# Filters of a Fourier mixer loaded over 128 partitions instead of 64

## The chip, the cores and the metric

The kernel runs on one core of a Trainium2 chip. The metric is the device time of one launch in microseconds (us). A core has five instruction queues that run side by side: TensorE (PE in the profile; PEld is its weight load), VectorE (DVE), ScalarE (ACT), GpSimd (POOL) and SyncE (SP). SP does no arithmetic; in this kernel it issues the plain DMA transfers, which 16 DMA engines carry out. Data lies in SBUF, which has 128 partitions; matmul results arrive in PSUM banks and are moved to SBUF ("evacuated") by DVE or ACT.

## The reference, cut to what matters

```python
# x: 8 batches x 2496 positions x 256 channels; filt_r, filt_i: 1249 frequencies x 256
X = np.fft.rfft(x, axis=1)
Y = X * (filt_r + 1j * filt_i)          # a complex filter for each frequency and channel
y = np.fft.irfft(Y, n=2496, axis=1)     # 19968 rows of 256
# then a mixture of 8 experts: each row goes to the expert with the largest gate logit
h = np.maximum(rows_of_e @ w1[e], 0.0)  # 256 -> 1024
out = gate * (h @ w2[e])                # 1024 -> 256
```

All of it is float32. The change concerns only how the filter gets into SBUF, which happens once, in the first 50 us.

## The kernel before, in words

The length 2496 is split as 39 x 64, so that a transform is a matmul with a 39-point table, a matmul with a 64-point table, the product with the filter, and the two inverse tables. A batch passes four stages: A (table `tas`, from x), B (table `tbs`, then the filter), C (table `tcs`) and D (table `tds`). Batch 0 keeps its intermediate results in SBUF and turns them with TensorE transposes; batches 1 to 7 go through DRAM between the stages (`zd` after A, `ud` after C). x is laid out in 22 columns of 128 partitions a batch and read in six chunks (`load_x`, L506): five of 512 KB and one of 256 KB. The expert products begin later, between the stages of the following batches, and fill most of the span.

After stage B's matmul a PSUM bank holds, for two of the `NF` = 20 frequency slots f, the real part on partitions 0 to 63 and the imaginary part on partitions 64 to 127. `stage_b` (L542) multiplies it on DVE and adds:

```python
nc.vector.tensor_mul(ys, z2, ht[:, f:f + 2, :])             # both halves times filt_r
... yw[:HP] = -z2[HP:] * fi ; yw[HP:] = z2[:HP] * fi        # crosswise times filt_i
nc.gpsimd.tensor_tensor(ys, ys, yw, op=ALU.add)             # batch 0, at times up to batch 2; else on DVE
```

So `filt_r` is needed alike on both halves, and `filt_i` on one half only, whose index is `f // 10`: `fi` for slots 0 to 9 lies on partitions 0 to 63, and for slots 10 to 19 on partitions 64 to 127. The tile `ht` (L366) holds both: columns 0 to 19 are `filt_r`, columns 20 to 29 are `filt_i` folded in this way. The filter in DRAM has the same shape (128 x 30 x 256), with `filt_r` present twice. For part of the frequencies `filt_i` must change its sign; the signs are in `sgs`, and GpSimd multiplies them in.

`load_filters(c)` (L419) is called five times, for chunks of four slots, each time between two chunks of `first_a` (L612, stage A of batch 0). It issues DMAs on SP and puts the sign products on a list. `turn_z(f)` (L628, the transposes between stage A and B of batch 0) starts, at every fourth f, with the copy of `filt_r` from the lower half to the upper on ACT, and with the sign products of the chunks up to one ahead.

What sets the order of the work: a planner written into the kernel (class `Order`) keeps an estimated clock for each engine, and picks the next step by when its inputs and banks are expected; all instructions are recorded through one helper, which is why nearly every row of the profile has the line L246. `Order.parts` (L152) splits `ht` into pieces for this estimate. `either` (L401) gives an evacuation to DVE or ACT, whichever is expected to end first. `more_loads` (L1288) issues the loads of x, `zd` and `ud`, at most seven tiles at a time (tile name `fin`). SP issues its DMAs strictly in order, and each waits for the landing of the eighth before it, besides what it needs itself.

Of the kernel before, what the change touches and what calls it, by code (L numbers as in the profile page):

```python
# [19 lines left out]
P = 128  # L20
S = 2496
D = 256
# [6 lines left out]
NF = (N1 + 1) // 2  # L29
# [95 lines left out]
class Order:  # L125
# [25 lines left out]
    @staticmethod  # L151
    def parts(a):  # L152

        if a.name[:3] != "ht_":
            return [a.name]
        row, at = divmod(a.offset, a.ap[0][0])
        return [f"{a.name}/{h}/{k}" for h in ((0, 1) if a.ap[0][1] == P else (row // (P // 2),))
                for k in range(at // (2 * D), at // (2 * D) + (a.ap[1][1] + 1) // 2)]

    @staticmethod  # L160
    def run(ap):
# [132 lines left out]
def kernel(  # L294
# [16 lines left out]
    nc = Order(tc.nc)  # L311
# [13 lines left out]
    for b in range(B):  # L325
        GROUPS.append([])
        for rows, most in WANT[b]:
            n = min(most, max(0, ((b + 1) * S - (N - left) - E * (rows - 1)) // rows))
# [35 lines left out]
    sgs = cst.tile([P, NF // 2], F32, name="sgs")  # L364

    ht = cst.tile([P, NF + NF // 2, D], F32, name="ht")  # L366
# [28 lines left out]
    def bank():  # L395
        return ps.tile([P, 512], F32, tag="bank", name="bank")
# [12 lines left out]
    def evac(o, i, n):  # L409
        either(i, n, lambda: nc.vector.tensor_copy(o, i), lambda: nc.scalar.copy(out=o, in_=i))  # L410

    HP = P // 2
# [4 lines left out]
    signs = []  # L417

    def load_filters(c):  # L419
        f0, n = FH[c]  # L420
        if c == 0:
            nc.sync.dma_start(out=tbs, in_=tb)
            nc.sync.dma_start(out=sgs, in_=sg)
        nc.sync.dma_start(out=ht[:HP, f0:f0 + n], in_=filt[:HP, f0:f0 + n, :])
        half, f1 = divmod(f0, NF // 2)
        rows = slice(half * HP, (half + 1) * HP)
        nh = min(n, NF // 2 - f1)
        parts = [(rows, slice(f1, f1 + nh), slice(NF + f1, NF + f1 + nh))]
        if nh < n:
            parts.append((slice(HP, P), slice(0, n - nh), slice(NF, NF + n - nh)))  # L430
        for r, fs, at in parts:
            nc.sync.dma_start(out=ht[r, at], in_=filt[r, at, :])
            signs.append((c, ht[r, at], sgs[r, fs, None].to_broadcast((HP, fs.stop - fs.start, D))))
        if c == 0:
            nc.sync.dma_start(out=tcs, in_=tcm)

# [190 lines left out]

    def turn_z(f):  # L628
        if f % 4 == 0:
            nc.scalar.copy(out=ht[HP:, f:f + 4], in_=ht[:HP, f:f + 4])  # L630
            while signs and signs[0][0] <= f // 4 + 1:
                _, part, sign = signs.pop(0)
                nc.gpsimd.tensor_tensor(part, part, sign, op=ALU.mult)
        zi = outs["zi", f] = pro.tile([P, 2, D], F32, tag="zi", name="zi")
        p = bank().rearrange("p (i h d) -> p i h d", i=2, h=DH)
        for i in range(2):
            for h in range(DH):
                nc.tensor.transpose(p[:, i, h, :], zu["z"][:, h, f + i].rearrange("p t c -> p (t c)"), ident)
        evac(zi, p.rearrange("p i h d -> p i (h d)"), 2 * D)
# [576 lines left out]
    def slot(k):  # L1216

        steps, nch = [], len(CH)
        if k == 0:
            steps.append((0.8, load_rest, None, 0.0, None))  # L1220
            for f in range(-2, NF + 2, 2):
                at = (f + 2) / (NF + 4)
                if 0 <= f < NF:
                    steps.append((at, lambda f=f: stage_b(k, f), None, 0.85, "b", lambda f=f: count("y") < 4 and [outs["zi", f]]))
                if f + 2 < NF:
                    steps.append((at + 0.01, lambda f=f: turn_z(f + 2), None, 0.44, "z", lambda: count("zi") < 2 and [zu["z"]]))
                if f >= 2:
                    steps.append((at + 0.02, lambda f=f: first_c(f - 2), None, 0.85, "c", lambda f=f: [outs["y", 0, f - 2]]))
        elif k < B:
            for f in range(0, NF + 4, 2):  # L1230
                at = f / (NF + 4)
                if f < NF:
                    steps.append((at, lambda f=f: stage_b(k, f), ("z", k, f // 4) if f % 4 == 0 else None, 0.85, "b", lambda f=f: count("y") < 4 and [ins["z", k, f // 4]]))
                if f >= 4:
                    steps.append((at + 0.01, lambda f=f: stage_c(k, f - 4), None, 0.85, "c", lambda f=f: [outs["y", k, f - 4], 0.0 if f % 4 else sb.free("st") - 0.9]))
# [31 lines left out]
        return sorted(steps, key=lambda step: step[0])  # L1267

    STEPS = [(0.0, lambda: load_filters(0), None, 0.0, None)]
    for c in range(len(CH)):  # L1270
        STEPS.append((0.0, lambda c=c: first_a(c), ("x", 0, c), 0.43 * CH[c][1], None))
        if c + 1 < len(FH):
            STEPS.append((0.0, lambda c=c: load_filters(c + 1), None, 0.0, None))
# [191 lines left out]
    with tc.manual_schedule(engines=None):  # L1465
# [4 lines left out]
        fs = list(STEPS)  # L1470
# [103 lines left out]
```

## Time and profile before

| what | value |
|---|---|
| three runs | 1468.29, 1470.89, 1471.23 us; median 1470.89 us |
| the profiled execution's own time | 1474.5 us |
| its span, first to last instruction | 1472.8 us |
| mean granted TensorE clock | 0.992 |
| HBM read / written | 196.45 MB / 80.64 MB |
| busy: DVE, ACT, POOL | 835.8, 480.5, 818.9 us |
| filter loads (`ht<-in_filt_dram`) | 11 DMAs from 8.5 to 28.0 us: nine of 256 KB, two of 128 KB |

How to read the profile: times are us from the first instruction; a row `out<-in` names the tile written and the tiles read; "idle before" is how long the engine had nothing to run, with the one that released it. The chain of waits follows the last instruction back to what let it start, again and again, so its pieces are the stretches that set the end. PEclk in a table of windows is the share of full clock that TensorE was granted. GB/s is what the 16 DMA engines moved together.

### The profile page before, as it was taken

How to read it: one execution, taken by the hardware profiler on the slowest of the kernel's cores; microseconds unless marked ns; L12 is line 12 of the kernel's file. 1: busy time of each engine (PE TensorE's matmuls, PEld its weight loads, DVE VectorE, ACT ScalarE, POOL GpSimd, SP SyncE). 2: the span in 40 equal slices, each digit the busy share in tenths (PEclk: the TensorE clock that was granted, in tenths of full speed). 3: DMA queues.
4: the chain of work that ended last, by engine and by line, in shares of the span. 5: the costliest groups of instructions: out<-in, count | busy, mean ns of one | idle time of the engine just before them, and what ended most of it. 6: DMA issues, size and time to landing. Idle time of an engine off the chain costs nothing.

```text
span 1472.8 us, 25703 instructions
## 1 busy us (share of the span) xinstructions
PE 1438.4 (98%) x7828; PEld 1148.5 (78%) x7828; DVE 835.8 (57%) x1818; ACT 480.5 (33%) x1005; POOL 818.9 (56%) x1214
## 2 busy tenths in 40 slices
PE   8998999999999999999999999999999999999998
PEld 5553555777577777777787778889999999999997
DVE  4666568335766574566757554566878775531110
ACT  3553443233232333222223232222232322223332
POOL 3434355525456654565375567647989878831111
PEclk9999999999999999999999999999999999999999
DMA  9749798887786576557345644548665424456661
GB/s 255 243 156 339 250 323 257 271 260 222 246 246 189 169 253 180 150 167 251 105 126 151 205 117 132 149 128 244 175 186 154 133 77 139 135 191 176 173 192 42
DMA packets 216383, 278.19 MB, mean 189 GB/s; under 512 B 124131, under 2 KB 163708, under 8 KB 216245
## 3 DMA queue, kind: packets, MB, share of 16 engines
q1 hardware_dynamic: 197125, 233.19, 53.7%
q0 software_dynamic: 19120, 43.33, 8.5%
q8 instruction: 66, 1.08, 0.3%
q14 instruction: 72, 0.59, 0.1%
HBM read 196.45 MB, written 80.64 MB: 188 GB/s over the span
## 4 chain that ended last, share of the span: by engine, by line
PE 85%; DMA 6%; DVE 4%; issue 2%; POOL 1%; SPq 1%; ACT 1%; POOLq 0%; DVEq 0%; ACTq 0%
PE bank L246 85%; DMA fin<-in_x_dram 2%; DMA fin<-ud 2%; DVE yw L246 1%; DVE ys L246 1%; DMA ud<-uo 1%; DMA fin<-zd 1%; SPq L246 1%; POOL out_dram L246 0%; DVE hT L246 0%; DMA w1t<-in_moe_w_dram 0%; DMA ng<-rows 0%; ACT hT L246 0%; DMA zd<-zo 0%; DMA xg<-rows 0%
## 5 line engine op out<-in xcount | busy, mean ns | idle before, releaser
L246 DVE TENSOR_TENSOR hT<-bank,hT 128x512 f32<-128x512 f32 (+1 forms) x504 | 300.8, 626 | 165.4 <-PE bank L246 77.7
L246 PE MATMUL bank<-w2t,hT 128*128 128x256 f32 (+1 forms) x1984 | 387.5, 350 | 2.4 <-DVE hT L246 1.4
L246 PEld LDWEIGHTS bank<-w2t,hT 128*128 128x128 f32 x1984 | 335.1, 190 | 53.0 <-issue 11.7
L246 PE MATMUL bank<-xT,w1t 128*128 128x256 f32 (+1 forms) x1728 | 316.3, 329 | 0.2 <-DVE hT L246 0.2
L246 POOL DMA_INDIRECT out_dram<-ys,ng x161 | 161.5, 1003 | 271.6 <-ACT ys L246 136.7
L246 PEld LDWEIGHTS bank<-xT,w1t 128*128 128x128 f32 x1728 | 265.4, 192 | 32.4 <-issue 8.3
L246 ACT ACTIVATE hT<-hT 128x1024 f32<-128x1024 f32 (+1 forms) x144 | 135.0, 959 | 390.5 <-DVE hT L246 387.5
L246 POOL DMA_INDIRECT rows<-yo,row x176 | 181.9, 1034 | 74.8 <-POOL yo L246 38.5
L246 ACT ACTIVATE ys<-bank,ng 128x256 f32<-128x256 f32 x104 | 49.3, 474 | 303.9 <-PE bank L246 235.2
L246 PE MATMUL bank<-sums,wsum 128*128 128x256 f32 (+1 forms) x576 | 135.6, 358 | 0.0
L246 PE MATMUL bank<-w2s,hT 128*128 x592 | 132.6, 379 | 0.0
L246 PEld LDWEIGHTS bank<-w2s,hT 128*128 128x128 f32 x592 | 110.3, 190 | 13.8
L246 PEld LDWEIGHTS bank<-sums,wsum 128*128 128x128 f32 x576 | 100.5, 190 | 17.7 <-issue 6.8
L246 POOL TENSOR_TENSOR wsum<-w1t 128x256 f32<-128x256 f32 x72 | 56.5, 785 | 82.2 <-PE bank L246 57.7
L246 DVE STREAM_TRANSPOSE xT<-xg 128x512 f32<-128x512 f32 (+2 forms) x126 | 57.4, 493 | 54.6 <-PE bank L246 51.4
L246 DVE TENSOR_TENSOR ys<-bank,ht 128x512 f32<-128x512 f32 x80 | 54.8, 685 | 52.2 <-PE bank L246 42.9
L246 PE MATMUL bank<-fin,tas 117*120 117x512 f32 x154 | 77.3, 622 | 6.9 <-DMA fin<-in_x_dram 6.7
L246 PE MATMUL bank<-fin,tds 120*128 120x512 f32 (+1 forms) x168 | 76.1, 573 | 3.9 <-DMA fin<-ud 3.3
L246 PE MATMUL bank<-fin,tbs 128*128 128x512 f32 x140 | 72.6, 605 | 5.4 <-DMA fin<-zd 5.4
L246 PE MATMUL bank<-ys,tcs 128*128 128x512 f32 x140 | 73.3, 611 | 4.2 <-DVE yw L246 3.4
L246 ACT ACTIVATE hT<-bank 128x128 f32<-128x128 f32 (+1 forms) x191 | 57.6, 303 | 52.5 <-PE bank L246 42.9
L246 PE MATMUL bank<-xT,wsum 128*128 128x256 f32 (+1 forms) x288 | 67.8, 358 | 0.2 <-ACT yo L246 0.2
(171 smaller groups left out, 1766.6 us busy)
## 6 DMA issues: line engine op xcount, KB each, us to landing
w1t<-in_moe_w_dram SPq DMA_DIRECT2D x126, 512.0 KB
w2t<-in_moe_w_dram SPq DMA_DIRECT2D x68, 512.0 KB
fin<-in_x_dram SPq DMA_DIRECT2D x39, 512.0 KB
fin<-zd SPq DMA_DIRECT2D x35, 512.0 KB
ud<-uo SPq DMA_DIRECT2D x35, 512.0 KB
fin<-ud SPq DMA_DIRECT2D x35, 512.0 KB
zd<-zo SPq DMA_DIRECT2D x35, 480.0 KB
xg<-rows SPq DMA_DIRECT2D x112, 128.0 KB
```

The lines of the kernel that those rows point to most:

```text
L246: return real(*args, **named)
```

## The change

`filt_r` is loaded onto all 128 partitions by DMA (512 KB a chunk instead of 256 KB), and ACT no longer copies it from the lower half. `filt_i` is loaded on all 128 partitions too, so a load of slots f brings the slots f + 10 with it: the three first chunks load it (512, 512 and 256 KB) and the last two load none. The signs are multiplied on 128 partitions, in three instructions instead of six. `Order.parts` no longer tells the halves of `ht` apart. `filt`, `ht` and `stage_b` stay as they are.

```diff
@@ class Order: parts
-        row, at = divmod(a.offset, a.ap[0][0])
-        return [f"{a.name}/{h}/{k}" for h in ((0, 1) if a.ap[0][1] == P else (row // (P // 2),))
-                for k in range(at // (2 * D), at // (2 * D) + (a.ap[1][1] + 1) // 2)]
+        at = a.offset % a.ap[0][0]
+        return [f"{a.name}/{k}" for k in range(at // (2 * D), at // (2 * D) + (a.ap[1][1] + 1) // 2)]
@@ load_filters
-        nc.sync.dma_start(out=ht[:HP, f0:f0 + n], in_=filt[:HP, f0:f0 + n, :])
-        half, f1 = divmod(f0, NF // 2)
-        rows = slice(half * HP, (half + 1) * HP)
-        nh = min(n, NF // 2 - f1)
-        parts = [(rows, slice(f1, f1 + nh), slice(NF + f1, NF + f1 + nh))]
-        if nh < n:
-            parts.append((slice(HP, P), slice(0, n - nh), slice(NF, NF + n - nh)))
-        for r, fs, at in parts:
-            nc.sync.dma_start(out=ht[r, at], in_=filt[r, at, :])
-            signs.append((c, ht[r, at], sgs[r, fs, None].to_broadcast((HP, fs.stop - fs.start, D))))
+        nc.sync.dma_start(out=ht[:, f0:f0 + n], in_=filt[:, f0:f0 + n, :])
+        nh = max(0, min(n, NF // 2 - f0))
+        if nh:
+            fs, at = slice(f0, f0 + nh), slice(NF + f0, NF + f0 + nh)
+            nc.sync.dma_start(out=ht[:, at], in_=filt[:, at, :])
+            signs.append((c, ht[:, at], sgs[:, fs, None].to_broadcast((P, nh, D))))
@@ turn_z
-            nc.scalar.copy(out=ht[HP:, f:f + 4], in_=ht[:HP, f:f + 4])
```

How the two built kernels compare, instruction by instruction: TensorE's list is the same. SP issues 8 filter loads instead of 11, in the same places between the other loads, which keep their order. ACT loses its five copies of `ht`. The planner's estimates shift a little with that, and `either` gives three evacuations of batches 0 and 1 to ACT that DVE had before. GpSimd has three sign products instead of six. In the kernel before the first two of them stand ahead of the sums `ys` of slots 0 and 2, two more ahead of those of slots 4 and 6, one ahead of slot 8 and one ahead of slot 12; in the changed kernel the first two stand at the same place and the third ahead of slot 4. Everything else on the five lists is the same and in the same order.

## Prediction

> **What bounds the kernel now.** I read the page first: section 1 (busy time) and section 4 (the chain that ended last). TensorE is busy 98% of the span and makes up 85% of the chain; no other engine makes up more than 4%.
>
> ```profile
> PE 1438.4 (98%) x7828; PEld 1148.5 (78%) x7828; DVE 835.8 (57%) x1818; ACT 480.5 (33%) x1005; POOL 818.9 (56%) x1214
> ...
> PE 85%; DMA 6%; DVE 4%; issue 2%; POOL 1%; SPq 1%; ACT 1%; POOLq 0%; DVEq 0%; ACTq 0%
> ```
>
> So taking work off ACT or GpSimd is worth nothing by itself. It counts only where it shortens a wait of TensorE. The filter is used from 19 us on and is complete by about 48 us; so I asked for the chain in order of time, up to 60 us.
>
> ```profile
> 8.48 3.76 PE bank L246 x32
> 12.24 10.14 DMA fin<-in_x_dram
> 22.38 0.14 issue
> 22.52 28.65 PE bank L246 x124
> ...
> 52.26 3.57 DMA zd<-zo
> ...
> 55.98 3.94 DMA fin<-zd
> ```
>
> The columns are start, length, what. One load stands out: `fin<-in_x_dram`, the second x chunk of batch 1. SP issues it at 12.24, and it lands at 22.38, 10.14 us later. TensorE stood idle for 2.92 us before it ("22.52 ... [2.92 <-DMA fin<-in_x_dram]" in the timeline). From 22.52 to 51.17 the chain is TensorE alone. The waits for `zd` at 52 to 60 are behind an ACT evacuation and SP, and begin from TensorE's results.
>
> Why 10 us for 512 KB? The busy times by window tell (columns: busy PE, PEld, DVE, ACT, POOL with counts, then PEclk, DMA share, GB/s):
>
> ```profile
> 8.00:12.00 4.00, 3.52 (x31) 3.52 (x32) 0.95 (x3) 1.13 (x3) 0.00 (x0) 1.00 1.01 398
> 12.00:16.00 4.00, 4.00 (x38) 4.00 (x38) 1.91 (x5) 1.59 (x5) 0.00 (x0) 1.00 1.08 234
> 16.00:20.00 4.00, 3.60 (x20) 2.19 (x18) 1.54 (x4) 2.41 (x5) 0.38 (x1) 1.00 1.03 226
> 20.00:24.00 4.00, 1.48 (x2) 0.80 (x3) 0.48 (x1) 0.41 (x1) 1.51 (x1) 0.73 1.03 224
> ...
> 60.00:64.00 4.00, 3.94 (x15) 2.26 (x16) 2.75 (x4) 1.07 (x2) 0.54 (x1) 1.00 1.03 409
> ```
>
> The DMA engines are full in all five rows. But with 128-partition loads alone (8 to 12 us: x; 60 to 64: x and `zd`) they move 398 and 409 GB/s, and once the 64-partition filter loads are among them, 224 to 234. The second thing to see is PEclk, which I asked for around the idle time:
>
> ```profile
> 18.39:21.80 3.41, 1.21 (x9) 0.80 (x7) 1.29 (x2) 1.73 (x3) 1.89 (x1) 1.00 1.03 214
> 21.80:28.63 6.83, 6.11 (x8) 2.48 (x9) 0.56 (x1) 2.21 (x3) 1.89 (x1) 0.50 1.05 245
> 28.63:58.00 29.37, 29.37 (x152) 19.45 (x150) 23.36 (x36) 17.63 (x34) 18.50 (x14) 1.00 0.70 185
> ```
>
> After 18.39 to 21.80, with TensorE busy for only 1.21 of 3.41 us, the clock is halved for 6.83 us. After 28.63 TensorE is busy without a gap to 58. Two later windows, for comparison:
>
> ```profile
> 124.20:127.62 3.42, 1.38 (x3) 0.30 (x2) 3.32 (x6) 1.45 (x3) 1.53 (x3) 1.00 1.03 339
> ...
> 260.74:264.15 3.41, 1.75 (x4) 0.42 (x3) 2.01 (x10) 2.38 (x9) 0.19 (x1) 1.00 1.00 330
> ```
>
> **The change part by part.**
>
> *Bytes.* Before: nine loads of 256 KB and two of 128 KB, 2.62 MB. After: five and two of 512 KB and one of 256 KB, 3.93 MB. Of the 1.31 MB more, 0.52 MB (the second halves of the chunk-0 `filt_r` and `filt_i`) stand on SP ahead of the x chunk that lands at 22.38; as much again (chunk 1) stands just behind it. What is that worth? Bounds from the rows: if 234 GB/s is all that this mix gets, 0.52 / 0.234 = +2.2 us. If the 64-partition loads are what makes it 234, and all runs at 398, then the 2.3 MB that moved from 12.24 to 22.38 (0.234 x 3.76 + 0.226 x 4 + 0.224 x 2.38) and the 0.52 MB more take 2.84 / 0.398 = 7.1 us instead of 10.14: -3.0 us. I take only the loads that certainly change: chunk 0's two, 0.52 MB at 0.234 = 2.24 us, become 1.05 MB at 0.398 = 2.63 us (+0.4); the x chunk itself, 0.52 MB, from 2.24 to 1.32 us (-0.9). Sum -0.5 us: it lands at 21.9.
>
> [...]
>
> *TensorE's clock.* The matmuls between 22.52 and 28.63 ran at half speed, so 6.11 us did 3.05 us of work. The slow stretch is 6.83 = 2 x 3.41 us long, and the others in this trace end on the same raster; so if the clock drops again, it comes back at 28.63 whenever TensorE starts. Starting 0.5 us earlier then gains 0.25 us. If the clock doesn't drop, the gain is 0.5 + 3.05 = 3.5 us. The drops in this trace came after 3.41 us windows with 1.21, 1.38 and (151.50 to 154.93) 1.39 us of work; none came after the window with 1.75. With the same raster, work from 22.04 on would still lie outside the window; it would have to start before 21.62 to come over 1.39. [...] The likelier is a drop, as before.
>
> *ACT.* Five copies of 1.04 us go, three evacuations of 0.6 to 0.7 us come from DVE. ACT is busy for 17.63 of 29.37 us from 28.63 to 58 and TensorE waits for it nowhere there: 0. If that cover were gone, at most the largest single wait on it, 0.7 us (PEld for ACT `zi`).
>
> *GpSimd.* Six sign products go (four of 1.89 us, two of 1.04), three come. The trace has no 128x1024 one. Nearest are the same on 64 partitions, 1.89 us, and `ys<-ys,yw`, 128x512 in 1.27 us against 1.04 for 64x512; so 1.89 to 2.31 us, and I take 2.1: 4 x 1.89 + 2 x 1.04 = 9.6 us become 2 x 2.1 + 1.2 = 5.4. The first two still stand ahead of the first `ys`. The second waits for chunk 1 of `filt_i`; it started at 24.71 and ended at 26.6, and `ys` could start at 30.24 only, because of DVE. Queued behind it: `ys`, then TensorE's stage C. So 3.6 us cover it: 0. If the clock stays fast, `ys` is wanted about 3.5 us earlier, the cover is used up, and up to 0.5 us is lost.
>
> *SP and the waits.* Three issues of 0.47 us go. Every later DMA waits for the eighth before it, which is now another one. There is slack for that: TensorE wants the next x chunk at 29.93, and it had landed by 26.69, when SP issued the filter load that waits for it: 0. DVE's first `ys` waits no more for ACT's copy, but TensorE's result for it came at the same time: 0.
>
> *After 60 us* the lists are the same, and each DMA wait on the chain begins from an instruction that moves along: 0, with the shift kept.
>
> Sum: -0.25 us on the profiled 1474.5 us (span 1472.8, 1.7 around it). That run is 3.6 us above the median; the difference is applied to the median: 1470.6.
>
> **The rivals.** 0.2% is 2.9 us, about what a measurement of this kernel can tell from no change.
>
> A, the forecast: loads a little better, clock still dropping. 1469.5 to 1471.5 us. Chance 48%.
>
> B, the clock is kept: the x chunk lands by 21.4 (the rates allow 19.4) or the raster is kinder: the 3.5 us above, up to 5 with the earliest landing, 1466 to 1467.4. For it: twice the bytes at nearly twice the rate. Against it: 0.5 us is not enough on this raster. 24%.
>
> C, slower: the mix doesn't speed up, because 224 to 234 GB/s comes from reading short rows in HBM and not from the half-filled partitions. Place: the queue ahead of the x chunk. It lands 2.2 us later, at 24.6; TensorE starts at 24.7, and until 28.63 does 1.95 instead of 3.05 us of work (+1.1); with 5.1 us idle the clock may come back one window later, another +1.7. The next x chunk, 4.5 us of extra bytes behind, lands at 31.2, and may cost up to 1 us against when it is then wanted. So +1.1 to +3.8, with the late window 2.8 to 3.8, say +3.3: 1474.2. It turns the sign once the x chunk lands after 22.4, and goes beyond 0.2% once the clock comes back a window later. For it: 1.31 MB more in a stretch with full DMA engines. Against it: 398 GB/s on the same queue just before. 28%, of which 4 stay within 0.2%.
>
> That the change doesn't do what it says is out: the instruction lists show the wider loads and no copy.
>
> **How the numbers follow.** Likeliest A, 1470.6. The range takes most of B and C: 1466.0 to 1474.7. Faster by over 0.2%: B, 24%; within: A and the small end of C, 52%; slower: 24%.
>
> **What would show it.** Right: GB/s near 400 from 12 to 20 us; the x chunk landing near 21.9; no ACT copy; sign products near 2.1 us; PEclk 0.50 for one or two windows after 22; the TensorE stretch from 29 to 58 without a gap. Wrong: GB/s still near 234, a landing after 22.4, or a full clock from 20 to 29 us.

## The result and the profile after

| | kernel before | changed kernel |
|---|---|---|
| median of the first 8 runs each | 1468.89 us (1467.28 to 1471.23) | 1465.35 us (1463.23 to 1470.01) |
| ratio, 95% interval | | 0.9969 (0.9956 to 0.9982) |
| mean of all runs in the comparisons | 1469.8 us (234 runs) | 1465.4 us (36 runs) |
| profiled execution: own time, span, clock | 1474.5, 1472.8, 0.992 | 1470.01, 1468.3, 0.994 |

The changed kernel is faster by 0.3%. By the means of all runs that is 4.3 us (plus or minus 0.8, from the spread of the runs). But the kernel before was itself about 1 us faster in two series of runs than in the other three; with each timing of the changed kernel set against the runs of before in its own series, it gains 3.5, 6.2 (6 runs only) and 3.2 us, 3.8 us on average (plus or minus 0.9). The forecast was 1470.6 us, no change, and its range began at 1466.0. One kernel's runs spread over some 15 us, and the profiled execution of before, at 1474.5, was one of its slowest. So a profile is read here for places and durations, and the sum is taken from the timed runs; a gain in us beside a ratio is that ratio of 1470 us.

The page of the changed kernel first, the line of busy times:

```profile
PE 1437.2 (98%) x7828; PEld 1148.7 (78%) x7828; DVE 836.4 (57%) x1815; ACT 476.6 (32%) x1003; POOL 814.5 (55%) x1211
```

ACT has 3.9 us less to do and GpSimd 4.4, DVE 0.6 more; TensorE is the bound as before. Now the windows that had shown the slow DMA (busy time of PE, PEld, DVE, ACT, POOL, then PEclk, DMA share, GB/s):

```profile
8.00:12.00 4.00, 3.67 (x33) 3.67 (x33) 1.52 (x4) 1.36 (x4) 0.00 (x0) 1.00 1.01 392
12.00:16.00 4.00, 4.00 (x38) 4.00 (x37) 1.75 (x5) 1.74 (x5) 0.00 (x0) 1.00 1.04 405
16.00:20.00 4.00, 4.00 (x21) 2.48 (x20) 1.43 (x3) 2.21 (x5) 1.89 (x1) 1.00 1.04 423
20.00:24.00 4.00, 4.00 (x17) 2.24 (x16) 2.10 (x4) 2.04 (x4) 1.90 (x1) 1.00 1.02 410
60.00:64.00 4.00, 4.00 (x13) 1.76 (x12) 0.83 (x2) 2.74 (x6) 1.44 (x2) 1.00 1.04 386
```

The last column is the change: 405, 423 and 410 GB/s where it was 234, 226 and 224. The DMA engines were full in both kernels (share 1.02 to 1.08); they were full of slower work before. TensorE's row at the second x chunk of batch 1 in the timeline of before, and its rows in that of the changed kernel (start, length, what):

```profile
22.52 3.74 PE L246 MATMUL bank<-fin,tas 117*120 117x512 f32 x4 [2.92 <-DMA fin<-in_x_dram]
...
18.18 1.04 PE L245 MATMUL bank<-ident,zt 128*128 128x128 f32 x8
19.06 1.88 PE L245 MATMUL bank<-fin,tas 117*120 117x512 f32 x4
20.78 1.88 PE L245 MATMUL bank<-zi,tbs 128*128 128x512 f32 x4
```

The four matmuls `bank<-fin,tas` on this chunk started at 22.52 after an idle time of 2.92 us; in the changed kernel they follow at 19.06 without one. They take 1.88 us instead of 3.74, because the clock is whole:

```profile
18.39:21.80 3.41, 3.41 (x15) 1.95 (x14) 0.69 (x1) 2.34 (x4) 1.46 (x2) 1.00 1.02 413
21.80:28.63 6.83, 6.83 (x36) 4.36 (x35) 6.56 (x10) 2.97 (x6) 4.53 (x5) 1.00 1.03 411
28.63:58.00 29.37, 27.61 (x137) 17.86 (x135) 19.92 (x31) 14.22 (x31) 11.15 (x9) 1.00 0.71 217
```

In the stretch from 21.80 to 28.63 TensorE is now busy for 6.83 us at full clock, where it was busy for 6.11 us at half clock, which is 3.05 us of work. (The counts, 36 matmuls against 8, can't be set side by side: many of the 36 are short ones.) The chunk was issued at 12.10 and its last piece arrived at 18.1 (before: 12.24 and 22.4). The next wait on the chain is for `fin<-zd`; it ends at 60.06 in before and at 53.37 in the changed kernel:

```profile
60.06 1.10 PE L246 MATMUL bank<-fin,tbs 128*128 128x512 f32 x2 [1.79 <-DMA fin<-zd]
...
53.37 1.10 PE L245 MATMUL bank<-fin,tbs 128*128 128x512 f32 x2 [1.76 <-DMA fin<-zd]
```

There this profile is 6.7 us ahead; at the end it is 4.5 ahead. One profile's lead at this place is a rough measure: it ended at 58.96 in the second profile of before, and at 53.64 and 57.02 in the second and third of the changed kernel.

### The profile page after: what moved, and what is told of

The parts are those of the page before. It is cut to its first block, busy times and chain, and to the rows that moved or that the text cites. A ratio compares the mean times of both kernels' runs of the same rounds, so it can differ in the third digit from the quotient of the medians.

```text
span 1468.3 us, 25687 instructions
## 1 busy us (share of the span) xinstructions
PE 1437.2 (98%) x7828; PEld 1148.7 (78%) x7828; DVE 836.4 (57%) x1815; ACT 476.6 (32%) x1003; POOL 814.5 (55%) x1211
## 3 DMA queue, kind: packets, MB, share of 16 engines
q8 instruction: 66, 1.08, 0.3%
```

## The experiments

Two theories stood at the start. **Ports** (a name only; no trace shows a port): a DMA whose SBUF side is one half of the partitions runs at about half the rate (224 to 234 GB/s with such loads in before, 398 without) and holds up whatever is in flight with it; so TensorE waits for an x chunk, and wide loads remove the wait. **Clock:** the wait matters mostly through the halved clock behind it. A third, **work**, says that the copies and sign products that went were the gain. The numbers of all profiles, sorted by GB/s (waits: TensorE waiting for x between 10 and 51 us):

| kernel | GB/s, 12 to 24 us | waits for x, us | ratio to before (95%) |
|---|---|---|---|
| before, second profile | 206 | 2.7 | 0.9993 (0.9981 to 1.0006) |
| clock kept in the gap | 222 | 0.3, rest filled | 1.0005 (0.9989 to 1.0021) |
| x chunk first | 222 | 3.3 | 0.9992 (0.9978 to 1.0006) |
| before, first profile | 228 | 2.9 | 1 |
| all loads in two halves | 252 | 3.4 | 1.0023 (1.0011 to 1.0035) |
| signed filters wide | 282 | 0.3 | 0.9993 (0.9984 to 1.0002) |
| first chunk wide | 287 | 1.5 | 0.9987 (0.9976 to 0.9999) |
| unsigned filters wide | 312 | 1.1 | 0.9980 (0.9970 to 0.9989) |
| first chunk in halves | 332 | 1.1 | 0.9982 (0.9972 to 0.9991) |
| two loads, every other partition | 386 | 0 | 0.9967 (0.9955 to 0.9979) |
| changed, second profile | 408 | 0 | 0.9950 (0.9938 to 0.9963) |
| changed, third profile | 408 | 0 | 0.9985 (0.9973 to 0.9997) |
| wide loads only | 410 | 0 | 0.9973 (0.9963 to 0.9984) |
| wide loads only, again | 412 | 0 | 0.9982 (0.9972 to 0.9991) |
| changed, first profile | 413 | 0 | 0.9969 (0.9956 to 0.9982) |
| changed, copies put back | 414 | 0 | 0.9978 (0.9965 to 0.9990) |

### The kernel before again

No edit.

> The kernel before, unchanged: a control, and a second profile of it. Every theory expects the ratio to the kernel before within 0.2% of 1. The port theory (a DMA whose SBUF side spans 64 partitions goes at half the rate and holds up what is queued with it) expects the second profile to repeat the first at the start: about 225 GB/s from 12 to 24 us, the x chunk of the second batch row landing near 22.4 us, a TensorE gap of about 3 us before it and two stretches of 3.41 us at the lower clock. If the start differs from run to run (landing earlier than 20 us, no drop of the clock), the 6.7 us by which the changed kernel led at 60 us were luck of one profile.

The time agrees with that of before. The start repeats in the wait, not in the clock. TensorE's row at the x chunk, in the timeline of this second profile of before:

```profile
23.62 1.95 PE L246 MATMUL bank<-fin,tas 117*120 117x512 f32 x4 [2.20 <-DMA fin<-in_x_dram]
```

and two of its windows:

```profile
20.00:24.00 4.00, 1.80 (x11) 1.18 (x10) 1.29 (x2) 1.94 (x3) 1.89 (x1) 1.00 1.02 205
24.00:28.00 4.00, 4.00 (x16) 2.06 (x14) 1.44 (x3) 2.45 (x4) 1.41 (x1) 1.00 1.05 207
```

The idle time is there (2.20 us) and so is the low rate (205 and 207 GB/s), but the clock stays at 1.00: this expectation of two slow stretches after it failed. (This profile had one earlier, from 8.83 to 12.25, at the end of the wait for the first x.) The chunk landed at 23.5, 1.1 us later than in the first profile. The 3.05 us that the prediction had tied to the halved clock belong to one execution, not to the kernel.

### The clock kept in the gap

```diff
@@ stage_a
+        if (b, c) == (1, 1):
+            idle = bank()
+            for _ in range(12):
+                tc.nc.tensor.matmul(idle[:, :TK], lhsT=ident[:TP], rhs=tas, start=True, stop=True)
```

> The kernel before with 12 more matmuls (ident by tas, 120 columns, into a bank that nobody reads) ahead of the first stage of the second batch row's second chunk, so that TensorE is busy in the gap of 3 us while it waits for the x chunk. The loads and the gap in useful work stay. Clock theory (what the change saved was mostly the two stretches of 3.41 us at half clock, worth about 3.4 us): the clock stays at 1.00 from 21.8 to 28.6 us, and the kernel is 3 to 4 us ahead at 60 us; at the end 2 to 4 us faster, ratio 0.9975 to 0.9985. If the wait itself is what counts (the late x chunk, 3 us), the ratio is 1.000 and the kernel at 60 us is less than 1 us ahead.

The timeline of TensorE in this kernel:

```profile
18.88 2.84 PE L536 MATMUL bank<-tas,ident 117*128 117x120 f32 x24
21.78 1.98 PE L246 MATMUL bank<-fin,tas 117*120 117x512 f32 x4
23.59 1.88 PE L246 MATMUL bank<-zi,tbs 128*128 128x512 f32 x4
```

The idle matmuls (the profile shows two for each of the 12) fill 18.88 to 21.72. The chunk landed at 21.1 in this execution; the real matmuls start at 21.78, so the filling itself held them up by about 0.6 us, and they run at full clock (1.98 us, not 3.74). The clock did what was asked, and the time did not: 1.0005, with a gain of more than 1.6 us outside the interval. The clock theory wanted 2 to 4 us. If the filling costs 0.6 us in every execution, up to 2.2 us of clock stay possible, its lowest end and no more.

One thing in this profile speaks for it: the wait for `fin<-zd` ends at 55.98, 4.1 and 3.0 us ahead of the two profiles of before, and the expectation had tied such a lead to the clock. Of these, 1.3 and 2.4 us are the chunk's own earlier landing in this execution, and the 14 timed runs show no gain. So the clock theory is not supported as the main cause, and a lead at 60 us in one profile is not a gain at the end.

Over all runs the mean granted clock is 0.9940 for before, 0.9944 for this kernel (and 0.9944 for the kernel before in its own repeat) and 0.9949 for the changed one. 0.0009 of 1467 us is 1.3 us; in the series with most runs of the changed kernel the difference is 0.0003, or 0.5 us. So, as an estimate, 0.5 to 1.3 us of the gain of some 4 can be clock, and no run shows at which gap.

### The wide loads alone, and the old work put back

Wide loads only: the kernel before, with

```diff
-        nc.sync.dma_start(out=ht[:HP, f0:f0 + n], in_=filt[:HP, f0:f0 + n, :])
+        nc.sync.dma_start(out=ht[:, f0:f0 + n], in_=filt[:, f0:f0 + n, :])
+        if f0 < NF // 2:
+            at = slice(NF + f0, NF + f0 + min(n, NF // 2 - f0))
+            nc.sync.dma_start(out=ht[:, at], in_=filt[:, at, :])
...
-            nc.sync.dma_start(out=ht[r, at], in_=filt[r, at, :])
```

> The kernel before with one part of the change: the filter loads on 128 partitions. The five ScalarE copies between the halves are kept (they copy into partitions that already hold the same numbers), and so are the six sign products of 64 partitions. Port theory: the x chunk lands near 18 us, GB/s from 12 to 24 us near 400, TensorE without a gap there and at full clock, some 6 to 7 us ahead of before at 60 us; in the end the whole gain of the change, 3 to 5 us (ratio 0.9965 to 0.998). Work theory (the gain comes from the copies and the three sign products that went): no change, ratio 1.000, within 0.2%, even if the loads land sooner.

Measured 0.9973, x landing at 18.8, 410 GB/s, no wait of TensorE for x after 10 us. SP's list is that of the changed kernel, every other engine's that of before. The work theory had 1.000. But the changed kernel, run again without an edit, gave a lower ratio than in its first timing:

> The changed kernel, unchanged: a second profile of it, and its time beside the same runs of the kernel before as the two other kernels here. Expected 0.9965 to 0.9978. If the copies and the sign products are worth nothing, it agrees within 0.1% with the 0.9973 of the kernel that only has the wide loads; if they are worth 1 us or more, it lies at 0.9965 or lower. In the profile: no gap of TensorE over 0.8 us between 9 and 50 us, the x chunk at 18 to 19 us.

It was 0.9950 from few runs, outside what was expected, which left room for 1 to 2 us from the work that went. So both kernels were compared in one series, with a third, the changed kernel with this line back in `turn_z`:

```diff
+            nc.scalar.copy(out=ht[HP:, f:f + 4], in_=ht[:HP, f:f + 4])
```

> The kernel before with all filter loads on 128 partitions and all of the old work (five copies, six sign products) kept, timed again beside the changed kernel. If copies and products cost nothing, within 0.1% of the changed kernel in the same comparison, both at 0.9955 to 0.9975; if they cost 1 to 2 us, 0.07 to 0.14% above it.

> The changed kernel once more, in the same comparison. 0.9955 to 0.997 by its two earlier timings. If copies and sign products cost nothing, the kernel with the wide loads alone gives the same within 0.1%.

> The changed kernel with the five ScalarE copies put back (they write what is already there); three sign products. ScalarE gets 5 copies of about 0.4 to 0.5 us more, 2 us in all between 18 and 45 us. If the copies are hidden, the changed kernel's time; if they were worth something, up to 1.5 us more (0.1%).

0.9982, 0.9985 and 0.9978: no order by the amount of work. The changed kernel's three timings (0.9969, 0.9950, 0.9985) differ more from each other than from these. The means of this series are 1467.1 us for the wide loads alone, 1465.8 for the changed kernel and 1465.7 with the copies back. With the copies back the planner also gave the three evacuations back to DVE. So copies and evacuations together are worth nothing that can be measured (-0.2 us, plus or minus 1.3). The copies took 1.04 us each, about twice what had been expected, and TensorE waited for none of them. By their lists of instructions the first kernel and the third differ only in the sign products, six against three: 1.4 us, plus or minus 1.5. The wide loads alone gained 4.0 and 2.0 us against before in their two series, so they carry most of the gain; whether the sign products add up to a us or so stays open.

Two halves of the wide loads, each with its own part of the work:

```diff
@@ unsigned filters wide: before, with
-        nc.sync.dma_start(out=ht[:HP, f0:f0 + n], in_=filt[:HP, f0:f0 + n, :])
+        nc.sync.dma_start(out=ht[:, f0:f0 + n], in_=filt[:, f0:f0 + n, :])
-            nc.scalar.copy(out=ht[HP:, f:f + 4], in_=ht[:HP, f:f + 4])
@@ signed filters wide: the changed kernel, with
-        nc.sync.dma_start(out=ht[:, f0:f0 + n], in_=filt[:, f0:f0 + n, :])
+        nc.sync.dma_start(out=ht[:HP, f0:f0 + n], in_=filt[:HP, f0:f0 + n, :])
+            nc.scalar.copy(out=ht[HP:, f:f + 4], in_=ht[:HP, f:f + 4])
```

> The kernel before with the unsigned filters loaded on 128 partitions and their ScalarE copies gone; the other filters still come in loads of 64 partitions with six sign products. About half of the filter bytes are still in narrow loads. Port theory: 300 GB/s or so from 12 to 24 us, the x chunk lands between 19 and 21.5 us, a gap of 0 to 2 us, and 1 to 3 us faster at the end (0.998 to 0.9993). Work theory (the copies on ScalarE were the cost): the full gain of 3.5 us, ratio 0.997 to 0.998, although the x chunk is late.

> The counterpart of the run with the unsigned filters wide: here the signed filters come in loads of 128 partitions with three sign products of 128 partitions, and the unsigned ones keep their loads of 64 partitions and the ScalarE copies. Port theory: half of the narrow bytes are left, so about 300 GB/s from 12 to 24 us and half of the gain, as in the counterpart: 1 to 3 us faster (0.998 to 0.9993). Work theory, GpSimd's side (the three sign products that went were the cost): the full gain, 0.997 or less.

0.9980 and 0.9993, or 2.9 and 1.0 us of 1470; together 3.9, near the whole. The larger gain goes with the higher rate (312 against 282 GB/s), but the two intervals overlap. The second one's interval reaches 1, so it shows no gain for certain; its small wait of 0.3 us is not typical, since TensorE was late by itself there, after a slow stretch of the clock at 8.84 to 12.25.

### Why a load of half the partitions is slow

Two edits of the changed kernel that move the same bytes in the same number of DMAs, of 64 pieces of 4 KB each (2 KB in the last signed load), and differ only in which partitions go together:

```diff
+    def two_loads(o, i):
+        nc.count("sync", "dma_start", (), dict(out=o, in_=i))
+        for r in (slice(0, HP), slice(HP, P)):              # all loads in two halves
+        for r in (slice(0, P, 2), slice(1, P, 2)):          # every other partition
+            tc.nc.sync.dma_start(out=o[r], in_=i[r])
...
-        nc.sync.dma_start(out=ht[:, f0:f0 + n], in_=filt[:, f0:f0 + n, :])
+        two_loads(ht[:, f0:f0 + n], filt[:, f0:f0 + n, :])
-            nc.sync.dma_start(out=ht[:, at], in_=filt[:, at, :])
+            two_loads(ht[:, at], filt[:, at, :])
```

> The changed kernel with each filter load split in two DMAs, one for partitions 0 to 63 and one for 64 to 127: the same bytes into the same places, no copies, three sign products. If the width of a single DMA sets its rate (port theory in its strict form), two loads of 64 partitions, run one after the other, keep 225 to 260 GB/s from 12 to 24 us, and as they now carry all the bytes the x chunk lands later than in the kernel before, at 23 to 26 us: 1 to 5 us slower than before (ratio 1.001 to 1.0035). If what counts is that both halves of the partitions are in use at the same time, the two loads overlap, GB/s is near 400, the x chunk lands near 18 us, and the time is that of the changed kernel, ratio 0.9965 to 0.998.

> The changed kernel with each filter load in two DMAs of 64 partitions, as in the run with two narrow loads, but one of the even partitions and one of the odd partitions instead of the lower and the upper half. Number, size and count of the DMAs are the same (64 pieces of 4 KB each). [...] Count theory (a DMA of 64 pieces is slower than one of 128 because of its pieces or its fixed part, wherever they lie): about 245 GB/s and 1.001 to 1.0035, as measured with the halves.

Lower and upper half, by windows:

```profile
12.00:16.00 4.00, 4.00 (x35) 4.00 (x35) 1.63 (x4) 1.53 (x5) 0.00 (x0) 0.94 1.07 265
16.00:20.00 4.00, 4.00 (x28) 3.16 (x27) 1.55 (x4) 1.88 (x5) 0.00 (x0) 1.00 0.99 246
20.00:24.00 4.00, 2.26 (x12) 1.37 (x11) 0.69 (x1) 1.28 (x3) 1.89 (x1) 1.00 1.03 245
```

Every other partition, the same windows:

```profile
12.00:16.00 4.00, 4.00 (x39) 4.00 (x38) 1.70 (x5) 1.83 (x5) 0.00 (x0) 1.00 1.04 386
16.00:20.00 4.00, 4.00 (x19) 2.33 (x18) 1.35 (x3) 2.18 (x5) 1.89 (x1) 1.00 0.99 379
20.00:24.00 4.00, 4.00 (x17) 2.16 (x16) 2.35 (x4) 2.12 (x4) 2.13 (x2) 1.00 0.99 392
```

265, 246, 245 against 386, 379, 392 GB/s, 1.0023 against 0.9967, with the DMA engines equally full. So it is not the 64 pieces, not the smaller DMA and not the reading of short rows in HBM; it is that the pieces lie in one half. (A half is also a different set of rows in HBM than every other row; no run keeps the rows and changes only the partitions.) A pair of loads, one to each half and issued one after the other, brings little: the pairs of halves reach 245 to 265 GB/s, against 224 to 234 and 177 to 237 in the two profiles of before. What in the chip makes a half slow, no trace shows.

In the profile of the pairs of halves the x chunk was issued at 15.98, behind more DMAs than in before (12.24), and landed at 22.8, which is not later than in before (22.4 and 23.5), though 23 to 26 had been expected, and the wait for `fin<-zd` ended at 59.10, level with before. TensorE waited for x for 3.4 us instead of 2.9 and 2.7. Where the kernel loses its 3.4 us is not shown by this profile.

### Which loads hold the chunk up

First chunk wide: the kernel before, with the two loads of chunk 0 on all partitions (the signed one loads the other half's slots too, which the later narrow load brings again). First chunk in halves: the changed kernel with the pairs of halves for chunk 0 only.

```diff
@@ first chunk wide
-        nc.sync.dma_start(out=ht[:HP, f0:f0 + n], in_=filt[:HP, f0:f0 + n, :])
+        nc.sync.dma_start(out=ht[:P if c == 0 else HP, f0:f0 + n], in_=filt[:P if c == 0 else HP, f0:f0 + n, :])
-            nc.sync.dma_start(out=ht[r, at], in_=filt[r, at, :])
+            w = slice(0, P) if c == 0 else r
+            nc.sync.dma_start(out=ht[w, at], in_=filt[w, at, :])
@@ first chunk in halves
+        for r in (slice(0, HP), slice(HP, P)) if first else (slice(0, P),):      # first: c == 0
```

> The kernel before with the two filter loads of chunk 0 alone on 128 partitions; the narrow loads of the chunks behind them, the copies and the sign products stay. These two loads are all the filters that are issued ahead of the x chunk of the second batch row. Prediction on record (loads ahead are what counts, +0.4 us for their bytes and -0.9 us for the chunk itself): lands 0.5 us earlier at most, near 21.9 us, the gap stays. Theory of the stragglers (a narrow load holds up some of the 16 engines, and the chunk waits for the last of them): with wide loads ahead the chunk lands near 18.5 to 19.5 us, the gap of TensorE is under 0.5 us; the later narrow loads still cost something at the following chunks. At the end 1 to 3.5 us faster (0.9977 to 0.9993).

> The changed kernel with the two filter loads of chunk 0 alone in two DMAs each, lower and upper half of the partitions; the loads of the chunks behind stay on 128. Counterpart of the run with only the first chunk wide, which kept part of the gain (0.9987). If loads ahead of the x chunk and loads behind it add up, this kernel lies where that sum says: the x chunk lands at 20 to 22 us, a gap of 1 to 2.5 us, after that no further gap; 1.5 to 2.5 us slower than the changed kernel, ratio to the kernel before 0.998 to 0.999. If the loads ahead alone set the time, it is as slow as the kernel with all loads in halves, 1.001 or more; if only the later loads count, it keeps the changed kernel's 0.997.

What TensorE waited for between 10 and 51 us (total, times, longest), first chunk wide:

```profile
PE bank L246 <- DMA fin<-in_x_dram: 1.5, 2, 0.8
```

First chunk in halves:

```profile
PE bank L245 <- DMA fin<-in_x_dram: 1.1, 1, 1.1
```

With chunk 0 wide the x chunk landed at 19.7, 2.7 and 3.8 us earlier than in the two profiles of before. A wait of 0.68 us was left there (under 0.5 had been expected), and one of 0.80 us came at the chunk after it, where the loads are still narrow. With chunk 0 in halves there is one wait at 19.74 to 20.84 and none later. The gains, 1.9 us (0.9987) and 2.6 us (0.9982), add up to 4.5, about the whole: within the noise (plus or minus some 1.5 us each) loads ahead and loads behind count about alike.

The x chunk ahead of all filter loads, everything else as before:

```diff
@@ load_x: a spare tile of the output's buffers
+        if (b, c) == (1, 1):
+            xt = sb.tile([P, 4, DR], F32, tag="y", name="yo", bufs=YB)
...
@@ more_loads
-        while todo and len(ins) < NIN and sb.free("in") <= ...
+        while todo and (todo[0] == ("x", 1, 1) or len(ins) < NIN and sb.free("in") <= ...
```

> The kernel before with one load moved: the x chunk (batch row 1, chunk 1) is issued ahead of the filter loads, into a spare tile of the output's buffers; all filter loads stay at 64 partitions. Theory of the late chunk (the change gains because this chunk no longer lands behind the narrow filter loads): the chunk lands before 17 us, TensorE has no gap between 18 and 24 us, and the 2 to 3 us of that gap are gained at once; as the later x chunks and filters still come at 220 to 240 GB/s, a part is lost again in the next gaps before 32 us. At the end 1 to 4 us faster (ratio 0.9975 to 0.9993). Rival (the whole early stage is bound by bytes at the narrow rate, so the order of two loads only moves the gap): a gap of 2 us or more turns up at another chunk before 32 us, and the ratio is 1.000, within 0.2%.

TensorE's rows in the timeline:

```profile
19.63 1.88 PE L246 MATMUL bank<-yo,tas 117*120 117x512 f32 x4
...
27.44 1.37 PE L246 MATMUL bank<-fin,tas 117*120 117x512 f32 x2 [3.34 <-DMA fin<-in_x_dram]
```

The moved chunk (`yo`) is no longer waited for, though it landed at 18.8, later than expected; the next x chunk is waited for instead, for 3.34 us. The time, 0.9992 (0.9978 to 1.0006), fits the theory of the late chunk (0.9975 to 0.9993) as well as the rival (1.000 within 0.2%) and can't tell them apart. The wait does: the rival was right that the order of two loads moves it to another chunk. The DMA engines were full from 16 to 32 us in this profile too, at 172 to 222 GB/s; the whole stage was short of DMA rate.

With all loads wide TensorE waits for no x chunk from 10 to 51 us, so faster filter loads would have no such wait left to shorten.

## Why the prediction was wrong

**What bounds the kernel: right.** Only TensorE's wait for one x chunk was put on the path, and there the gain lies.

**Bytes and landing: the step that failed.** The prediction had the x chunk 0.5 us earlier (between 3.0 earlier and 2.2 later); it came 4.3 us earlier (18.1 instead of 22.4). It counted "only the loads that certainly change", at the mean rate, plus the chunk itself. The run with these two loads alone wide shows that the pricing failed and not only the count: they alone brought 2.7 us. Against the second profile of before, where the chunk landed at 23.5, they brought 3.8. A mean rate was the wrong measure for a landing. In the completion marks of the 16 DMA engines for this chunk the first engine was done at 17.4 in before and at 16.4 in the changed kernel, 1.0 us apart; the last at 22.4 and 18.1. The spread fell from 5.0 to 1.8 us, and a chunk has landed when the last engine is done. In before 15 of the 16 were done by 20.3, so the last 2.1 us of TensorE's wait were for a single engine; in the second profile of before four engines ended only at 23.0 to 23.5. The bound of 3.0 us was too tight as well: it let all bytes that were in flight be moved ahead of the chunk (2.84 MB), but in the 6.0 us that the chunk took, 405 to 423 GB/s move some 2.5 MB. ("Twice the bytes" in rival B holds for the loads of the first two chunks; over all five the bytes are one and a half times as many, as the prediction's own 2.62 and 3.93 MB say.)

**TensorE's clock: wrongly weighed.** "The likelier is a drop" fell with the landing: TensorE was busy from 18.39 to 28.63 in the changed kernel, and PEclk stayed at 1.00. The prediction's limit of TensorE's work in a window, between 1.39 and 1.75 us, was that of one trace: in the profile of the changed kernel a halved stretch followed a window with 1.70 us of work (126.59 to 130.00), and none followed windows with 1.65 (51.50 to 54.91) and 1.42 (170.97 to 174.38). The drop was also priced from one execution, at 3.05 us, as most of rival B; the second profile of before had the wait without a drop, and filling the gap gained nothing measurable. Rival B's condition, a landing by 21.4, came true, and it had nearly the right total (3.5 to 5 us), but its split was wrong, so the total was in part luck: its 0.5 us of waiting and 3.05 of clock are rather, as an estimate, some 3 us of waiting (2.7 to 2.9 in two profiles) and 0.5 to 1.3 of clock.

**The rate of wide loads: right, if low.** The prediction took 398 GB/s for them, from before's 8 to 12 us; the changed kernel moves 405 to 423 GB/s from 12 to 24 us.

**GpSimd: right, size off.** The product on 128 partitions was put at 2.1 us. The groups of the changed kernel:

```profile
L245 POOL TENSOR_TENSOR ht<-ht,sgs 128x1024 f32<-128x1024 f32 x2 | 3.8, 1894 | 15.2 <-DMA ht<-in_filt_dram 15.2
L245 POOL TENSOR_TENSOR ht<-ht,sgs 128x512 f32<-128x512 f32 x1 | 1.0, 1039 | 0.0
```

and of before:

```profile
L246 POOL TENSOR_TENSOR ht<-ht,sgs 64x1024 f32<-64x1024 f32 x4 | 7.6, 1892 | 19.2 <-DMA ht<-in_filt_dram 19.1
```

1.894 and 1.892 us: twice the partitions cost nothing. The second product ran from 20.68 to 22.57 and the first `ys` of GpSimd at 24.0, so the cover held. The 0.5 us feared for it did not come.

**ACT and SP: 0, as far as this can be told** (the changed kernel with and without the copies, 1465.7 and 1465.8 us in one series).

**After 60 us: "the shift kept" held only roughly.** In this pair of profiles 6.7 us at 60 became 7.7 at 238, 6.4 at 258 (the wait for `fin<-zd` there was 3.84 us, against 2.43) and 4.7 at 837. The last step is one stretch of the clock in the changed kernel, which before did not have there:

```profile
259.70:263.11 3.41, 3.41 (x10) 2.69 (x9) 3.29 (x8) 0.00 (x0) 0.00 (x0) 0.50 1.02 416
```

TensorE is busy through all of it at half clock, which costs 1.7 us. The halved stretches of the first 300 us begin elsewhere in each of the two (at 21.80, 127.62, 154.93 and 247.08 in before, at 123.17, 130.00, 239.22 and 259.70 in the changed kernel), so this belongs to these two executions.

**Rival C fell at its reason:** the low rate does not come from reading short rows in HBM, as the pair of runs with equal pieces shows (245 to 265 against 379 to 392 GB/s). With all the changed kernel's bytes in halves the kernel is slower than before (1.0023), by 3.4 us, about the 3.3 that it had worked out; but the chunk landed at 22.8 there and not at 24.6, and no halved clock followed, so the equal size is luck, and how those 3.4 us arise stays open.

## What to carry to other kernels

When DMA engines are full and GB/s is low, look which partitions the transfers in flight cover: here one and a half times the bytes over all partitions landed sooner (the last filter load at 28.8 us) than the smaller load over one half (36.3), and the transfers beside them landed sooner too (the x chunk at 18.1 instead of 22.4). Price a landing by its last engine (22.4 in before, when 15 of 16 were done by 20.3), not by the mean rate; and before a cause that one profile shows (here the halved clock) is given a price, look whether a second profile of the same kernel has it.

## What had not been expected of the hardware

With 64-partition filter loads that cover every other partition the early stage moved 379 to 392 GB/s, nearly as much as with 128 partitions (405 to 423), and 245 to 265 with those that cover a half; the prediction had not told these two kinds of narrow load apart. A transfer issued ahead of the narrow loads landed late too: `tbs`, issued at 5.7 us in before and 2.8 us ahead of the first filter load, landed at 17.0, and at 14.1 in the changed kernel, where it was issued later, at 6.4. And the clock was halved near the very start, for 3.41 or 6.83 us beginning between 8.6 and 9.3 us, about when the wait for the first x ended; it was so in five of the 16 profiles, two of them of kernels whose filter loads are all wide.
